# Rounding float64 weights on VectorE in pairs of operations, each pair ordered behind an hl, with a third load buffer

## The chip, the cores and the metric

One core of one Trainium2 chip runs the whole program. The metric is device time in microseconds. The kernel before was timed three times: 1932.73 us in the median, 1931.42 the lowest and 1937.19 the highest. One further execution was taken with the hardware profiler; all rows shown here come from it.

## The reference

Three stages run one after the other on 4608 tokens (8 batches of 576) of width 512.

```python
# attention: softmax of q over its last axis, of k over the sequence; out = q_s @ (k_s^T @ v)
# mixture of experts: 8 experts, the two best per token
h = np.maximum(x[mask] @ w1[e], 0.0)                       # w1[e]: 512 x 1024
out[mask] += top2_w[mask, k, None] * (h @ w2[e])           # w2[e]: 1024 x 512
# second MLP, on all tokens; w_in 512 x 2048 and w_out 2048 x 512 arrive as float64
h = x @ w_in
g = h * np.cos(h)
return (g @ w_out).astype(np.float32)
```

w_in and w_out are float64 since they are scaled by a NumPy float. The kernel reads them as pairs of 32-bit words and rounds them to float32 itself, with integer and float operations on VectorE. That rounding is what the change touches.

## The kernel before

**Arithmetic.** Every large product is made of three matmuls on float32r operands: high part times high part, low part times high part, high part times low part (`xh`, `xl` the input's parts, `w1h`, `w1l`, `w2h`, `w2l` the weights', `hh`, `hl` the hidden layer's). ScalarE (ACT) makes a high part by a copy, VectorE (DVE) or GpSimd (POOL) the low part by a subtraction.

**Stages.** Attention and routing take the first quarter of a millisecond. Then come the eight experts. The tokens of an expert are gathered in blocks of 128 rows and worked on in groups: for expert 0 groups of 2, 2, 2 and 3 blocks, for each other expert groups of 4, 3 and 2. A tenth block (`last_block`) stands in a branch that is taken only where the expert has so many tokens. The second MLP (nine groups of four blocks, "moe2") follows.

**A step.** Each expert group takes eight steps, one for each 128 hidden columns. Step f issues `mm1` (lines 745 to 764): 12 matmuls into `ph`, then ACT's relu into `hh` (L756), then DVE's `hl` (L757). `mm2` (lines 766 to 776) of a step is issued two steps later (`LAG = 2`), so TensorE (PE) has about two steps in which `hh` and `hl` may come. At the end of a group the accumulators are copied out to `ys`, the even ones on ACT (L785), the odd ones on DVE (L787), and only then may the next group's `mm2` write those PSUM banks.

**Beside each step.** Three side lines advance step by step as Python generators. `fetch` gathers the next group's rows by indirect DMA on POOL (L618) and has SP's queue spread each block in four DMAs (L645). `prep` then turns a block on DVE (L677, here called T), rounds it on ACT (L680) and subtracts on DVE (L681, here x). `w_load` brings the next expert's weights in 16 pieces: a DMA on SP into one of three `wst` buffers (L141), a copy on ACT (L136), a subtraction on POOL (L137). `convert` is the fourth line and rounds the float64 weights.

**convert.** Lines 810 to 852. There are 64 jobs of 128 x 256 numbers, 32 of w_in and 32 of w_out. A job is a load on SP (L844, 256 KB into one of two buffers `c64`, which the trace calls c), seven or eight small DVE operations on `ca` and `cb` (L821 to L825 and L831 to L833), and a store on SP (L834) to `wi_d` or `wo_d` in DRAM, from where moe2's `w_load` reads. The trace's lines of one job are, in this order, L821, L822, L823, L824, L825, L831, L832, L833: eight operations.

**What sets the order.** The program is built with a scheduler that simulates the engines' time: it puts each engine's instructions in a fixed order, and may put an instruction earlier than the Python code does where its inputs allow. Each engine, and each engine's DMA queue, then works strictly in that order: an instruction that waits holds up all behind it. `tc.issue_after(ins)` adds an edge on the same engine, so that what stands in the block comes behind `ins`; `prep` uses it for T. `after` is the list of all `hl` instructions. `convert` has no such edge.

**Buffers.** `GB` are two 128 x 512 float32 tiles, `GB[0]` and `GB[1]` (gb in the trace). Up to moe2 only `last_block` uses them, in turns, for 128 columns each (L707).

Of the kernel before, what the change touches and what calls it, by code (L numbers as in the profile page):

```python
# [10 lines left out]
F32 = mybir.dt.float32  # L11
F32R = mybir.dt.float32r
BF16 = mybir.dt.bfloat16
I32 = mybir.dt.int32
U32 = mybir.dt.uint32
AF = mybir.ActivationFunctionType
ALU = mybir.AluOpType
# [4 lines left out]
P = 128  # L22
# [5 lines left out]
def tile_attention_moe_moe2(  # L28
# [669 lines left out]
    def last_block(g):  # L698

        w1h, w1l, w2h, w2l = W[g.e % 2]  # L700
        hs = []

        def up(f):
            fs = slice(f * P, (f + 1) * P)
            ph = ps_tr("ph")
            hh, hl = HH[f % (LAG + 1)][:, LASTB], HL[f % (LAG + 1)][:, LASTB]
            t = GB[f % 2][:, :P]  # L707
            if g.nb == 2:
                for kc in range(NK):
                    nc.tensor.matmul(ph[:, :2 * P], w1h[:, kc, fs], g.xh[:, kc, 2 * P:], start=kc == 0, stop=False)  # L710
                    nc.tensor.matmul(ph[:, :P], w1l[:, kc, fs], g.xh[:, kc, 2 * P:3 * P], start=False,
                                     stop=kc == NK - 1)
                nc.scalar.activation(t, ph[:, P:2 * P], AF.Copy)
                nc.vector.tensor_tensor(t, ph[:, :P], t, op=ALU.add)
            else:
                for kc in range(NK):
                    nc.tensor.matmul(ph[:, :P], w1h[:, kc, fs], g.xh[:, kc, LASTB], start=kc == 0, stop=False)
                    nc.tensor.matmul(ph[:, :P], w1h[:, kc, fs], g.xl[:, kc, LASTB], start=False, stop=False)
                    nc.tensor.matmul(ph[:, :P], w1l[:, kc, fs], g.xh[:, kc, LASTB], start=False, stop=kc == NK - 1)
                nc.vector.tensor_copy(t, ph[:, :P])  # L720
            nc.scalar.activation(hh, t, AF.Relu)
            nc.vector.scalar_tensor_tensor(hl, t, 0.0, hh.bitcast(F32), op0=ALU.max, op1=ALU.subtract)
            hs.append((hh, hl))

        def down(f):
            hh, hl = hs[f]
            nc.tensor.matmul(acc, hh, w2h[:, f, :], start=f == 0, stop=False)
            nc.tensor.matmul(acc, hh, w2l[:, f, :], start=False, stop=False)
            nc.tensor.matmul(acc, hl, w2h[:, f, :], start=False, stop=f == NF - 1)

        with tc.If(used[g.e] > 0):
            acc = ps_acc("acc")
            for f in range(NF + LAG):
                if f < NF:
                    up(f)
                if f >= LAG:
                    down(f - LAG)
            ys = YS[0]
            nc.scalar.activation(ys, acc, AF.Copy)
            nc.scalar.dma_start(y_rows(g.e, NB - 1), ys)  # L740
# [67 lines left out]
    EMAX = float(2 ** 16 * (1 + 7 / 8 - 2.0 ** -23))  # L808

    def convert():  # L810
        pend = []
        V = nc.vector

        def half1():
            src, t, dst = pend[0]
            v2 = t.rearrange("p (n w) -> p n w", w=2)
            lo, hi = v2[:, :, 0].bitcast(U32), v2[:, :, 1]
            ab = late[1].tile([P, CW], I32, name="ca", bufs=3)
            bits = late[1].tile([P, CW], I32, name="cb", bufs=1)

            V.tensor_single_scalar(ab, hi, 0x7fffffff, op=ALU.bitwise_and)  # L821
            V.tensor_scalar(ab.bitcast(F32), ab.bitcast(F32), EMIN, EMAX, op0=ALU.max, op1=ALU.min)  # L822
            V.tensor_scalar(bits, ab, 5, 2, op0=ALU.logical_shift_left, op1=ALU.logical_shift_right)  # L823
            V.scalar_tensor_tensor(bits, ab, 0x40000000, bits, op0=ALU.bitwise_and, op1=ALU.bitwise_or)  # L824
            V.scalar_tensor_tensor(bits, hi, -2 ** 31, bits, op0=ALU.bitwise_and, op1=ALU.bitwise_or)  # L825
            return lo, bits, ab

        def half2(lo, bits, ab):
            dst = pend.pop(0)[2]
            w = ab.bitcast(F32)  # L830
            V.tensor_single_scalar(ab, bits, -2 ** 23, op=ALU.bitwise_and)  # L831
            V.scalar_tensor_tensor(w, lo, 2.0 ** -52, w, op0=ALU.mult, op1=ALU.mult)  # L832
            V.tensor_tensor(w, w, bits.bitcast(F32), op=ALU.add)  # L833
            nc.sync.dma_start(dst, w)  # L834

        jobs = []
        for src, dst in ((w_in, wi_d), (w_out, wo_d)):
            s32 = src.bitcast(I32)
            for r in range(0, src.shape[0], P):
                for c in range(0, src.shape[1], CW):  # L840
                    jobs.append((s32[r:r + P, 2 * c:2 * (c + CW)], dst[r:r + P, c:c + CW]))
        for src, dst in jobs:
            t = late[1].tile([P, 2 * CW], I32, name="c64", bufs=2)
            nc.sync.dma_start(t, src)  # L844
            pend.append((src, t, dst))
            if len(pend) == 2:
                yield
                z = half1()
                yield
                half2(*z)  # L850
        yield
        half2(*half1())

    C2 = 2.0 * math.pi - C1
    MAGIC = 1.5 * 2.0 ** 23
# [29 lines left out]
    def experts():  # L885
# [4 lines left out]
        for i in range(first, len(steps) + LAG):  # L890
# [39 lines left out]
                if f == g.nf - 1:  # L930
                    finish(pbg)
            wbg.step(2 if g.t is not None or g.e == 0 else 1)
            if g.nb > 2 or f < p0:
                cbg.step(2 if f == 0 else 1)
            if f == g.nf - 1 and nxt is not None:
                if nxt.t == 0:
                    cbg.drain()
# [217 lines left out]
```

## Time and profile before

| | |
|---|---|
| median of three runs | 1932.73 us |
| profiled execution, device time | 1936.69 us |
| its span, first to last instruction | 1934.6 us |
| PE busy | 1815.6 us, 94% |
| DVE busy | 1118.6 us, 58% |
| ACT busy | 860.6 us, 44% |
| POOL busy | 447.7 us, 23% |
| mean granted TensorE clock | 0.962 |
| DMA, mean over the span | 107 GB/s |

PE is the busy engine, so the places that matter are those where PE stands idle or where its granted clock is under full. The page's forty slices show 8s and 9s for PE between 260 and 700 us, the stretch in which the 64 jobs run, and only 9s (90% or more) from there to the last slice. Idle time of another engine costs nothing by itself; it counts only through what PE then waits for.

### The profile page before, as it was taken

The page shows a single profiled execution, that of the slowest core. Times are in us where ns is not written, and L with a number is a line of the kernel's source. Part 1 is how long each engine was busy: PE and PEld are TensorE (multiplying, and loading weights), DVE is VectorE, ACT ScalarE, POOL GpSimd, SP SyncE. Part 2 cuts the span into 40 slices and gives each one's busy share as a digit, 9 for nine tenths or more (in the row PEclk, how much of TensorE's full clock was granted, in tenths as well). Part 3 has the DMA queues.
Part 4 walks back from the last instruction along what each step waited for, and adds up shares of the span by engine and source line. Part 5 has one row for each costly group of instructions (what it writes and reads, how often), then busy time and mean ns, then how long its engine had stood idle before and what let it go on. Part 6 is the DMA issues. An engine that isn't in the chain of part 4 may idle for free. (4 is left out here: it accounts for less than half of the span.)

```text
span 1934.6 us, 27003 instructions
## 1 busy us (share of the span) xinstructions
PE 1815.6 (94%) x9738; PEld 1531.3 (79%) x9738; DVE 1118.6 (58%) x2138; ACT 860.6 (44%) x1514; POOL 447.7 (23%) x405
## 2 busy tenths in 40 slices
PE   5875988999899999999999999999999999999998
PEld 4764877788787788888888878888888888888886
DVE  4657677877767744334323357665656566665654
ACT  5542223313123132232424256666666666666654
POOL 6655033404114023041405143110101010110000
PEclk8775999999999999999999999999999999999999
DMA  9954246546545443252435342211212030201000
GB/s 269 291 168 129 79 128 206 186 142 192 150 125 182 141 132 115 79 155 81 133 92 148 98 139 65 71 28 60 56 33 66 23 88 16 72 28 49 1 23 23
DMA packets 179774, 206.18 MB, mean 107 GB/s; under 512 B 34224, under 2 KB 121264, under 8 KB 179632
## 3 DMA queue, kind: packets, MB, share of 16 engines
q1 hardware_dynamic: 160704, 152.17, 26.4%
q0 software_dynamic: 12160, 39.86, 7.1%
q10 hardware_dynamic: 6768, 12.32, 1.7%
q8 instruction: 82, 1.34, 0.3%
q14 instruction: 60, 0.49, 0.1%
HBM read 127.06 MB, written 49.43 MB: 91 GB/s over the span
## 5 line engine op out<-in xcount | busy, mean ns | idle before, releaser
L750 PE MATMUL ph<-xh,w1h 128*128 128x512 f32 (+2 forms) x1376 | 491.9, 357 | 6.9 <-DVE r L696 2.9
L752 PE MATMUL ph<-xh,w1l 128*128 128x512 f32 (+2 forms) x1376 | 491.3, 357 | 0.0
L751 PE MATMUL ph<-xl,w1h 128*128 128x512 f32 (+2 forms) x1376 | 490.6, 357 | 0.0
L774 PE MATMUL acc<-w2h,hh 128*128 128x512 f32 x1152 | 455.8, 396 | 17.1 <-DVE ys L787 9.7
L775 PE MATMUL acc<-w2l,hh 128*128 128x512 f32 x1152 | 453.3, 394 | 0.0
L776 PE MATMUL acc<-w2h,hl 128*128 128x512 f32 x1152 | 427.7, 396 | 21.5 <-DVE hl L757 19.7
L750 PEld LDWEIGHTS ph<-xh,w1h 128*128 128x128 f32 x1376 | 261.8, 190 | 47.1 <-DVE hl L757 4.0
L751 PEld LDWEIGHTS ph<-xl,w1h 128*128 128x128 f32 x1376 | 261.5, 190 | 38.2 <-DMA xl<-xg 0.8
L752 PEld LDWEIGHTS ph<-xh,w1l 128*128 128x128 f32 x1376 | 261.8, 190 | 32.1
L776 PEld LDWEIGHTS acc<-w2h,hl 128*128 128x128 f32 x1152 | 217.2, 190 | 73.7 <-DVE hl L757 26.1
L774 PEld LDWEIGHTS acc<-w2h,hh 128*128 128x128 f32 x1152 | 218.2, 189 | 65.7 <-ACT hh L756 11.1
L775 PEld LDWEIGHTS acc<-w2l,hh 128*128 128x128 f32 x1152 | 218.4, 190 | 40.4
L757 DVE SCALAR_TENSOR_TENSOR hl<-ph,hh 128x256 fp32r<-128x256 f32 (+2 forms) x200 | 107.1, 538 | 243.3 <-ACT hh L756 243.1
L756 ACT ACTIVATE hh<-ph 128x256 fp32r<-128x256 f32 (+2 forms) x200 | 93.9, 472 | 265.2 <-PE ph L752 250.8
L696 DVE SCALAR_TENSOR_TENSOR r<-r,ph 128x512 f32<-128x512 f32 x144 | 98.9, 687 | 151.4 <-ACT r L695 150.3
L618 POOL DMA_INDIRECT xg<-x_d,idx x80 | 76.8, 959 | 441.8 <-DVE xl L681 190.4
L694 ACT ACTIVATE r<-r 128x512 f32<-128x512 f32 x144 | 90.7, 630 | 151.9 <-DVE r L693 151.9
L763 DVE TENSOR_TENSOR hl<-r,hh 128x512 fp32r<-128x512 f32 x144 | 102.1, 709 | 86.4 <-ACT hh L762 86.3
L680 ACT ACTIVATE xh<-xg 128x512 fp32r<-128x512 f32 x106 | 66.7, 630 | 166.2 <-DVE xg L677 164.0
L137 POOL TENSOR_TENSOR w1l<-wst,w1h 128x512 fp32r<-128x512 f32 x80 | 104.9, 1326 | 137.9 <-ACT w1h L136 137.0
L618 POOL DMA_INDIRECT xg<-y_d,SL x36 | 34.3, 954 | 420.5 <-DVE xl L681 389.8
L692 DVE SCALAR_TENSOR_TENSOR r<-kk,ph 128x512 f32<-128x512 f32 x144 | 98.7, 685 | 51.6 <-ACT kk L691 50.0
(186 smaller groups left out, 2162.9 us busy)
## 6 DMA issues: line engine op xcount, KB each, us to landing
wst<-in_moe_w_dram SPq DMA_DIRECT2D x128, 256.0 KB
xl<-xg SPq DMA_DIRECT2D x396, 64.0 KB
y_d<-ys ACTq DMA_DIRECT2D x47, 256.0 KB
kt<-in_k_dram SPq DMA_DIRECT2D x16, 512.0 KB
vt<-in_v_dram SPq DMA_DIRECT2D x16, 512.0 KB
qt<-in_q_dram SPq DMA_DIRECT2D x16, 512.0 KB
x_d<-xs SPq DMA_DIRECT2D x32, 256.0 KB
c<-in_moe_w_in_dram SPq DMA_DIRECT2D x32, 256.0 KB
```

What stands on the lines that cost most here:

```text
L137: nc.gpsimd.tensor_tensor(lo, st, hi.bitcast(F32), op=ALU.subtract)
L618: return nc.gpsimd.indirect_dma_start(out=dst, out_offset=None, in_=src, in_offset=bass.IndirectOffsetOnAxis(ap=ix, axis=0))
L692: nc.vector.scalar_tensor_tensor(r, kk, -C1, ph, op0=ALU.mult, op1=ALU.add)
L696: nc.vector.scalar_tensor_tensor(r, r, 1.0, ph, op0=ALU.subtract, op1=ALU.mult, reverse0=True)
L750: nc.tensor.matmul(ph, w1h[:, kc, fs], g.xh[:, kc, :g.N], start=kc == 0, stop=False)
L751: nc.tensor.matmul(ph, w1h[:, kc, fs], g.xl[:, kc, :g.N], start=False, stop=False)
L752: nc.tensor.matmul(ph, w1l[:, kc, fs], g.xh[:, kc, :g.N], start=False, stop=kc == NK - 1)
L757: after.append(nc.vector.scalar_tensor_tensor(hl, ph, 0.0, hh.bitcast(F32), op0=ALU.max, op1=ALU.subtract))
L763: after.append(nc.vector.tensor_tensor(hl, r, hh.bitcast(F32), op=ALU.subtract))
L774: nc.tensor.matmul(g.acc[m], hh[:, ms], w2h[:, fr, :], start=f == 0, stop=False)
L775: nc.tensor.matmul(g.acc[m], hh[:, ms], w2l[:, fr, :], start=False, stop=False)
L776: nc.tensor.matmul(g.acc[m], hl[:, ms], w2h[:, fr, :], start=False, stop=f == g.nf - 1)
```

## The change

The eight operations of a job are issued in four pairs instead of five and three. Each pair stands in a block `held()`, an edge behind the newest `hl` that has been issued. The generator gives up control after every pair. The jobs' number, the eight operations and their sizes stay as they were. A job's store is issued after the next job's first pair. Three loads are issued at the start and then one after each job; every third of them goes to `GB[0]` (which moe2 needs later), so that there are three buffers. `last_block` now uses two halves of `GB[1]`. The rate of the generator is set anew: one to three pairs for each step, in every step of every group.

```diff
-            t = GB[f % 2][:, :P]
+            t = GB[1][:, f % 2 * P:f % 2 * P + P]
...
-        for src, dst in jobs:
-            t = late[1].tile([P, 2 * CW], I32, name="c64", bufs=2)
-            nc.sync.dma_start(t, src)
-            pend.append((src, t, dst))
-            if len(pend) == 2:
-                yield
-                z = half1()
-                yield
-                half2(*z)
-        yield
-        half2(*half1())
...
+        def load():
+            n = next(loads)
+            if n < len(jobs):
+
+                t = GB[0].bitcast(I32) if n % 3 == 2 else late[1].tile([P, 2 * CW], I32, name="c64", bufs=2)
+                nc.sync.dma_start(t, jobs[n][0])
+                ring.append(t)
+
+        def held():
+
+            return tc.issue_after(after[-1].ins)
+
+        for _ in range(3):
+            load()
+        yield
+        for _, dst in jobs:
...
+            with held():
+                V.tensor_single_scalar(ab, hi, 0x7fffffff, op=ALU.bitwise_and)
+                V.tensor_scalar(w, w, EMIN, EMAX, op0=ALU.max, op1=ALU.min)
+            yield
+            if store is not None:
+                nc.sync.dma_start(*store)
+            with held():
+                V.tensor_scalar(bits, ab, 5, 2, op0=ALU.logical_shift_left, op1=ALU.logical_shift_right)
+                V.scalar_tensor_tensor(bits, ab, 0x40000000, bits, op0=ALU.bitwise_and, op1=ALU.bitwise_or)
+            yield
+            with held():
+                V.scalar_tensor_tensor(bits, hi, -2 ** 31, bits, op0=ALU.bitwise_and, op1=ALU.bitwise_or)
+                V.tensor_single_scalar(ab, bits, -2 ** 23, op=ALU.bitwise_and)
+            yield
+            with held():
+                V.scalar_tensor_tensor(w, lo, 2.0 ** -52, w, op0=ALU.mult, op1=ALU.mult)
+                V.tensor_tensor(w, w, bits.bitcast(F32), op=ALU.add)
+            store = (dst, w)
+            load()
+            yield
+        nc.sync.dma_start(*store)
...
-            if g.nb > 2 or f < p0:
-                cbg.step(2 if f == 0 else 1)
+            busy = f < LAG or (nxt is not None and p0 <= f < p0 + nxt.nx)
+            cbg.step((1 if g.nb == 2 or f < LAG else 2) if busy else 2 if g.nb == 2 else 3)
```

Counted over the program, the jobs' operations stood, before, from the early groups of expert 0 to the end of expert 3. Now the first pair stands behind the last `hl` of expert 0, and the last pair behind the last `hl` of expert 6's three-block group.

Three places in the engines' order show the move. The first is DVE in the four-block group of expert 1, from one hl to the next but for the first three operations of before (hl_1679 to hl_1680; L821 to L833 are the rounding's operations before, L843 to L858 the same ones now). Before:

```order
L822 TENSOR_SCALAR ca<-ca 128x256
L831 TENSOR_SCALAR ca<-cb 128x256
L832 SCALAR_TENSOR_TENSOR ca<-c_4483,ca 128x256
L833 TENSOR_TENSOR ca<-ca,cb 128x256
L823 TENSOR_SCALAR cb<-ca 128x256
L824 SCALAR_TENSOR_TENSOR cb<-ca,cb 128x256
L825 SCALAR_TENSOR_TENSOR cb<-c_4559,cb 128x256
L831 TENSOR_SCALAR ca<-cb 128x256
L821 TENSOR_SCALAR ca<-c_4858 128x256
L832 SCALAR_TENSOR_TENSOR ca<-c_4559,ca 128x256
L822 TENSOR_SCALAR ca<-ca 128x256
L757 SCALAR_TENSOR_TENSOR hl_1680<-ph,hh_1677 128x512
```

Now, the same two hl:

```order
L757 SCALAR_TENSOR_TENSOR hl_1679<-ph,hh_1676 128x512
L843 TENSOR_SCALAR ca<-c_3625 128x256
L844 TENSOR_SCALAR ca<-ca 128x256
L849 TENSOR_SCALAR cb<-ca 128x256
L850 SCALAR_TENSOR_TENSOR cb<-ca,cb 128x256
L853 SCALAR_TENSOR_TENSOR cb<-c_3625,cb 128x256
L854 TENSOR_SCALAR ca<-cb 128x256
L757 SCALAR_TENSOR_TENSOR hl_1680<-ph,hh_1677 128x512
```

Between these two hl stood 14 operations of the rounding; there are 6 now, and nowhere between two hl are there more than 6.

The second place is DVE at the end of that group, in the second step of the three-block group behind it, where `ys` is copied out (L787). Before:

```order
L757 SCALAR_TENSOR_TENSOR hl_1680<-ph,hh_1677 128x384
L821 TENSOR_SCALAR ca<-c_5321 128x256
L787 COPY ys_1683<-acc 128x512
L822 TENSOR_SCALAR ca<-ca 128x256
L821 TENSOR_SCALAR ca<-c_5396 128x256
L823 TENSOR_SCALAR cb<-ca 128x256
L822 TENSOR_SCALAR ca<-ca 128x256
L787 COPY ys_1681<-acc 128x512
```

Now:

```order
L757 SCALAR_TENSOR_TENSOR hl_1680<-ph,hh_1677 128x384
L843 TENSOR_SCALAR ca<-gb_3105 128x256
L787 COPY ys_1683<-acc 128x512
L844 TENSOR_SCALAR ca<-ca 128x256
L787 COPY ys_1681<-acc 128x512
```

A job's first operation, which needs its load, still stands ahead of the first ys copy; a second job's first operation no longer stands ahead of the second one.

The third place is SP's queue at the same point of the program (the loads are L844 and now L825, the stores L834 and now L847, L645 the spreading of gathered rows, L790 the stores of ys). Before:

```order
L834 DMA wi_d<-ca 128x256
L645 DMA xl_1690<-xg_1686 32x4x128 x4
L645 DMA xl_1690<-xg_1687 32x4x128 x4
L645 DMA xh_1689<-xg_1688 32x4x128 x4
L834 DMA wi_d<-ca 128x256
L844 DMA c_5321<-in_moe_w_in_dram 128x512
L834 DMA wi_d<-ca 128x256
L844 DMA c_5396<-in_moe_w_in_dram 128x512
L790 DMA y_d<-ys_1683 128x512
```

Now:

```order
L825 DMA gb_3105<-in_moe_w_in_dram 128x512
L847 DMA wi_d<-ca 128x256
L825 DMA c_4081<-in_moe_w_in_dram 128x512
L847 DMA wi_d<-ca 128x256
L645 DMA xl_1690<-xg_1686 32x4x128 x4
L645 DMA xl_1690<-xg_1687 32x4x128 x4
L645 DMA xh_1689<-xg_1688 32x4x128 x2
L825 DMA c_4161<-in_moe_w_in_dram 128x512
L645 DMA xh_1689<-xg_1688 32x4x128 x2
L847 DMA wi_d<-ca 128x256
L790 DMA y_d<-ys_1683 128x512
```

Before, the load that the operation ahead of the ys copy reads (c_5321) stood behind the twelve DMAs of L645; now the one that it reads (gb_3105) stands ahead of them, and one more load with it.

## Rows read from the trace of the kernel before

**Rows 1.** The page: the span of the profiled execution

```profile
span 1934.6 us, 27003 instructions
```

**Rows 2.** Stretches: length, busy us (instructions) per engine, granted clock, DMA share, GB/s

```profile
264.00:309.00 45.00, 36.07 (x208) 30.38 (x206) 36.12 (x64) 14.27 (x28) 27.41 (x24) 1.00 0.63 204
309.00:338.00 29.00, 25.55 (x110) 22.50 (x111) 20.46 (x47) 6.66 (x13) 5.26 (x6) 0.88 0.68 222
338.00:460.00 122.00, 112.13 (x530) 94.52 (x531) 94.22 (x198) 32.28 (x61) 34.40 (x29) 0.96 0.54 166
402.00:450.00 48.00, 48.00 (x259) 43.27 (x259) 36.95 (x93) 9.58 (x20) 5.24 (x6) 0.95 0.44 136
460.00:580.00 120.00, 111.42 (x569) 95.91 (x568) 87.37 (x205) 31.11 (x66) 26.45 (x23) 0.97 0.51 152
580.00:700.00 120.00, 110.47 (x548) 93.74 (x547) 85.14 (x197) 31.98 (x64) 30.49 (x26) 0.97 0.51 158
700.00:820.00 120.00, 120.00 (x639) 105.42 (x638) 42.05 (x74) 37.62 (x80) 30.00 (x26) 1.00 0.34 103
```

**Rows 3.** PE's waits, 264 to 700 us: waiting, released by, us, times, longest

```profile
PE acc L776 <- DVE hl L757: 19.7, 13, 3.5
PE acc L774 <- DVE ys L787: 9.7, 3, 3.7
PE acc L774 <- ACT hh L756: 6.1, 7, 1.7
PE ph L750 <- DVE hl L757: 2.7, 3, 1.4
PE pt L671 <- DMA xg<-x_d,idx: 1.3, 1, 1.3
```

**Rows 4.** DVE in order of time: start, us, operation [idle before, releaser]

```profile
400.17 0.29 DVE L821 TENSOR_SCALAR ca<-c 128x256 int32<-128x256 int32 x1 [5.58 <-DMA c<-in_moe_w_in_dram]
400.38 0.68 DVE L787 COPY ys<-acc 128x512 f32<-128x512 f32 x1
```

**Rows 5.** SP's DMA issues in order of time, same place

```profile
387.14 5.81 SPq L645 DMA_DIRECT2D xl<-xg  x8
...
396.21 0.46 SPq L844 DMA_DIRECT2D c<-in_moe_w_in_dram  x1
```

**Rows 6.** DVE's waits for the loads, 264 to 700 us

```profile
DVE ca L821 <- DMA c<-in_moe_w_out_dram: 33.9, 23, 5.4
...
DVE ca L821 <- DMA c<-in_moe_w_in_dram: 29.6, 17, 5.6
```

**Rows 7.** Two of the eight operations: ns min/median/max, first and last start

```profile
L824 DVE SCALAR_TENSOR_TENSOR cb<-ca,cb x64: 370/426/3314, 265.8 to 692.6; 128x256 int32<-128x256 int32 x64
L831 DVE TENSOR_SCALAR ca<-cb x64: 252/289/4440, 267.1 to 694.0; 128x256 int32<-128x256 int32 x64
```

**Rows 8.** DVE in order of time, one operation

```profile
365.05 4.44 DVE L831 TENSOR_SCALAR ca<-cb 128x256 int32<-128x256 int32 x1
```

**Rows 9.** POOL in order of time, same stretch

```profile
364.42 1.10 POOL L618 DMA_INDIRECT xg<-x_d,idx  x1 [3.46 <-DVE xl L681]
365.53 1.31 POOL L137 TENSOR_TENSOR w1l<-wst,w1h 128x512 fp32r<-128x512 f32 x1
366.78 2.55 POOL L137 TENSOR_TENSOR w2l<-wst,w2h 128x512 fp32r<-128x512 f32 x2
```

**Rows 10.** DVE in order of time, one step of a two-block group, no rounding

```profile
1021.28 1.13 DVE L677 STREAM_TRANSPOSE xg<-xl 128x512 f32<-128x512 f32 x1
1023.11 0.69 DVE L681 TENSOR_TENSOR xl<-xg,xh 128x512 fp32r<-128x512 f32 x1 [0.70 <-ACT xh L680]
1023.82 0.42 DVE L757 SCALAR_TENSOR_TENSOR hl<-ph,hh 128x256 fp32r<-128x256 f32 x1
```

More of the change, by code (lines that the diff above doesn't have):

```diff
@@ L810, in convert @@
     def convert():
-        pend = []
         V = nc.vector
[L814 to L834, printed above, removed]
         jobs = []
@@ L841, in convert @@
                     jobs.append((s32[r:r + P, 2 * c:2 * (c + CW)], dst[r:r + P, c:c + CW]))
-        for src, dst in jobs:
-            t = late[1].tile([P, 2 * CW], I32, name="c64", bufs=2)
-            nc.sync.dma_start(t, src)
-            pend.append((src, t, dst))
-            if len(pend) == 2:
-                yield
-                z = half1()
-                yield
-                half2(*z)
-        yield
-        half2(*half1())
+        ring, loads, store = [], itertools.count(), None
+        def load():
[8 more added lines that the diff above has]
+            load()
+        yield
+        for _, dst in jobs:
+            v2 = ring.pop(0).rearrange("p (n w) -> p n w", w=2)
+            lo, hi = v2[:, :, 0].bitcast(U32), v2[:, :, 1]
+            ab = late[1].tile([P, CW], I32, name="ca", bufs=3)
+            bits = late[1].tile([P, CW], I32, name="cb", bufs=1)
+            w = ab.bitcast(F32)
+            with held():
[19 more added lines that the diff above has]
+        nc.sync.dma_start(*store)
     C2 = 2.0 * math.pi - C1
```

## The prediction

> **What bounds the kernel now.** I read the page first, then the table by stretches, then PE's waits, and last DVE and SP in order of time around the longest of them. The span is 1934.6 us [rows 1] and PE is its bound, so only time that PE loses can be won. The table by stretches [rows 2] shows where it loses any. In 700 to 820, an expert with no rounding beside it, PE is busy for 120.00 of 120 us at a granted clock of 1.00. In the five stretches from 264 to 700 it is idle for 8.93 + 3.45 + 9.87 + 8.58 + 9.53 = 40.4 us (length less PE's busy time), and the clock is under 1.00 in four of them. PE at a mean clock c does c of the work, so that costs 0.12 x 29 + 0.04 x 122 + 0.03 x 120 + 0.03 x 120 = 15.6 us. Together 56.0 us, and that is the most that this change can give back, since the 64 jobs run nowhere else.
>
> PE's waits in the same stretch [rows 3] name what it waited for: hl 19.7 and 2.7, the ys copy 9.7, hh 6.1, a gather 1.3. All but the last come from DVE or from ACT. DVE is not full: 94.22 of 122 us, against 42.05 of 120 without the rounding [rows 2]. So it isn't DVE's mean load, it is what stands ahead of an hl or a ys at the wrong moment. Two forms of it can be read.
>
> The first is a load that DVE waits for. At 400.17 DVE had been idle for 5.58 us for a load, at the head of a job, and the ys copy stood right behind that operation [rows 4]. The longest of PE's three waits for ys, 3.7 us [rows 3], is this one. SP shows why: its load went out at 396.21, behind the issues of L645, eight of which alone began at 387.14 and took 5.81 us [rows 5]. DVE waited for loads 33.9 + 29.6 = 63.5 us in 40 cases [rows 6].
>
> The second is mere number. An interval between two hl held up to 14 operations of 0.29 to 0.43 us each [rows 7], some 5 us, beside T, x and hl, and any of them could be drawn out: the one at 365.05 took 4.44 us [rows 8] in place of 0.29, and it ended as three POOL subtractions ended that began behind a gather (365.53 to 369.33) [rows 9].
>
> **The change, part by part.**
>
> *Number and work.* 64 jobs of eight operations before and after, so DVE's work is the same. Rounding took some 174 us of DVE: 323.3 us busy in the five stretches less 42.05/120 of their 436 us. Spread over experts 1 to 6, that is 29 us for each; with 40 of its own, DVE is busy for about 69 us of an expert's 115, 60%. In 402 to 450 DVE was at 36.95 of 48, 77%, and PE was busy for all of it; only the clock was at 0.95, behind the stall at 400 us [rows 2, 4]. So the new density by itself lies under one that PE has been seen to bear.
>
> *The edge and the pairs.* At most 6 operations now stand between two hl, some 2.2 us at 0.29 to 0.43 [rows 7]. An hl has about two steps until PE needs it. The undisturbed cost is thus hidden by that slack. The tightest place is the two-block group, into whose last steps the change newly puts pairs. There DVE without rounding runs T 1.13, waits 0.70 for ACT, x 0.69, hl 0.42: a step of 2.88 us from hl to hl less the overlap of neighbours, and DVE is what paces it [rows 10]. A pair takes 0.58 to 0.85 us and stands between T and x, so it falls into the 0.70 us that DVE idles there: at most 0.15 us a step, four steps a group, which the slack takes up. If that cover were gone (the pair ahead of T instead), it would be 0.7 x 4 = 2.8 us for each expert.
>
> *Drawn-out operations.* These stay: w_load's 16 subtractions on POOL still fall into the four-block group, with up to six operations beside each. Price for an expert from below: 0, as in 700 to 820. From above: the loss of the three experts that had rounding before, (9.87 + 8.58 + 9.53 + 4.9 + 3.6 + 3.6) / 3 = 13.4 us. By the order, the four-block group of expert 1 has 34 operations where it had 66, and no late load among them; I take 1 us, near the lower row, so 6 us for six experts. The Trainium skill, "SBUF — State Buffer", section "SBUF: two separate sides", speaks of the pair of ports that DVE and GpSimd share as an exclusive lock held for one whole instruction. By that, an operation of DVE would lose no more than the rest of one POOL instruction, 1.3 us, every interval would fit into its step, and the six experts would cost 0 instead of 6: 1880. The trace differs: 4.44 us is three of POOL's instructions in a row [rows 8, 9], so the measured length holds in my sum.
>
> *The third buffer and SP.* A load is now issued at the end of a job for the third one after, so it goes out some eight pairs ahead of its use, which at one to three pairs a step is at least three steps. Landing takes about 4 us (issued 396.21, used 400.17 [rows 4, 5]). In SP's order the load for the operation ahead of the ys copy stands in front of L645's twelve DMAs. So the 63.5 us of DVE's waits should nearly go, and the 9.7 us for ys with them. Loads and stores on SP keep their number and size. What comes late next is the weights' own chain (SP, ACT, POOL) with hh behind it on ACT: 6.1 us of PE's waits, partly there without any rounding in the way; I leave it in the 1 us for each expert.
>
> *The early groups and the clock.* Nothing of the rounding is left ahead of expert 0's last hl but three loads. Of the 12.4 us idle there the gather's 1.3 stays, and about as much again for ACT waiting for weights: 3 us. The clock is under 1.00 only in stretches with some per cent of PE idle or right behind them, and 1.00 in 700 to 820 [rows 2]; without the idle time I let it cost nothing.
>
> *last_block* in halves of one tile: same operations, same lengths, 0. The bound is one wait of a small operation in each of 8 columns and 4 experts, 0.3 x 32 = 10 us, if the two halves waited for each other; their instructions wait for the same engines as before, so I take 0.
>
> *Sum.* 1936.7 us (the profiled execution) - 56.0 + 6 + 3 = 1889.7. That execution lies 4.0 us above the median of the three runs, so against the median 1886.
>
> **Rivals.** *Half comes back.* Drawn-out operations and ACT's waits for weights cost each of six experts about 5 us with the clock, as hh's and half of hl's waits did (6.1 + 11 us over some three and a half experts [rows 3]): 6 x 5 in place of 6, so 1910. For it: the POOL chain is untouched, and three experts more carry the rounding. Against it: 402 to 450.
>
> *Slower, by the head of a job.* A pair that waits for its load holds up hl and ys behind it, now in six experts. If SP stays behind with its L645 issues, so that loads still come late by 5.58 us ahead of ys in every expert, each loses what the three lost, 13.4: 6 x 13.4 + 3 - 56 = +27, 1960. It decides from (56 - 3) / 6 = 8.8 us for each expert. Against it: the load's new place in SP's order, and that the first three experts can hardly lose as much with half the operations.
>
> *It does nothing.* The scheduler could have kept the old density; the order shows that it hasn't. The time would be 1933.
>
> **The numbers.** Forecast 1886 with 0.72; half back 0.20; slower 0.04; nothing 0.04. The range goes from 1878 (1 us lost in all) to 1912, with the half-back case's 1910 in it. A difference under 0.3% (6 us) can't be told from no change. Faster 0.92, same 0.04, slower 0.04.
>
> **What would show it.** Right: in 264 to 1030 of the new profile PE idle in all under 12 us, clock 1.00 in each expert, DVE's wait for loads under 10 us, no wait for ys over 1 us, DVE near 60% in experts 1 to 6. Drawn-out operations will still be there, but PE doesn't wait for them. Wrong: waits of PE for hl in the four-block groups of experts 4 to 6, where there were none; the clock at its lower level (1.2 GHz) behind them; a head operation idle for a load ahead of ys.

## The result, and the profile after

The changed kernel takes 1886.02 us in the median (1881.85 to 1887.52) against 1933.51 (1931.42 to 1937.19) for the kernel before, taken again beside it: a ratio of 0.9749, 95% interval 0.9733 to 0.9766. The profiled execution took 1886.52 us. The page gives its span, 49.9 us less than [rows 1]:

```profile
span 1884.7 us, 27071 instructions
```

The table by stretches, with the columns of [rows 2]. The six stretches from 336.20 on are experts 1 to 6, each from its first hl to the next expert's; the jobs now stand there:

```profile
264.00:309.00 45.00, 40.54 (x237) 36.53 (x235) 7.89 (x18) 15.88 (x31) 27.93 (x24) 0.96 0.61 183
...
336.20:434.30 98.10, 97.95 (x496) 85.09 (x495) 66.64 (x137) 29.69 (x56) 30.05 (x26) 1.00 0.53 162
434.30:547.70 113.40, 113.40 (x597) 99.54 (x597) 70.18 (x152) 35.25 (x72) 29.59 (x27) 1.00 0.47 144
547.70:660.30 112.60, 112.60 (x594) 98.84 (x593) 70.39 (x153) 35.26 (x72) 30.76 (x28) 1.00 0.48 146
660.30:772.80 112.50, 112.50 (x594) 98.76 (x593) 69.95 (x152) 35.34 (x72) 30.10 (x27) 1.00 0.48 147
772.80:886.50 113.70, 113.70 (x599) 99.71 (x598) 70.25 (x153) 35.41 (x72) 31.58 (x28) 1.00 0.47 146
886.50:984.70 98.20, 98.05 (x497) 85.19 (x496) 58.98 (x116) 30.00 (x55) 29.89 (x27) 1.00 0.49 151
...
1080.00:1115.00 35.00, 28.19 (x118) 21.25 (x117) 19.00 (x20) 24.08 (x42) 25.76 (x22) 1.00 0.66 188
```

PE is busy for all but 0.15 us at most of each of these experts, where [rows 2] had 8.58 to 9.87 us of idle time in each of experts 1 to 3, and the clock is 1.00 in each. DVE is busy for 68% of expert 1 (66.64 of 98.10 us) and for 60 to 63% of the others. Nearly all idle time that is left ahead of expert 7 is the 4.46 us in the first row, and there the clock is at 0.96.

PE's waits from 260 to 1130 us (waiting, released by, us, times, longest), to be laid beside [rows 3]:

```profile
PE ph L750 <- DVE r L696: 4.1, 3, 2.8
PE acc L774 <- ACT hh L756: 3.2, 2, 2.7
PE acc L774 <- ACT hh L762: 1.7, 1, 1.7
PE pt L671 <- DMA xg<-x_d,idx: 1.3, 1, 1.3
PE acc L776 <- DVE hl L763: 0.9, 1, 0.9
```

The waits for an hl of L757 and for ys, 19.7, 2.7 and 9.7 us in [rows 3], have no row any more; hh is down from 6.1 to 3.2 us. The rows for r, for the other hh (L762) and for the other hl (L763) belong to moe2.

The place of [rows 4], DVE in order of time at the first ys copies of expert 1:

```profile
376.98 0.28 DVE L843 TENSOR_SCALAR ca<-gb 128x256 int32<-128x256 int32 x1
377.37 0.69 DVE L787 COPY ys<-acc 128x512 f32<-128x512 f32 x1
...
378.75 0.69 DVE L787 COPY ys<-acc 128x512 f32<-128x512 f32 x1 [0.48 <-PE acc L776]
```

The job's first operation still stands ahead of the copy, but it no longer waits for its load. Nor does any other: DVE's waits for the loads, 63.5 us in [rows 6], have no row in this trace. The drawn-out operations are still there, as this group shows beside the one of [rows 7] (ns min/median/max):

```profile
L854 DVE TENSOR_SCALAR ca<-cb x64: 286/294/1384, 337.4 to 954.6; 128x256 int32<-128x256 int32 x64
```

Its longest took 1.38 us, where 4.44 us stood before. Counted over all operations of the rounding, 31 lasted over 0.4 us longer than the median of their form (33 before), but none lasted over 1.7 us (9 before).

The following times between stages are differences of the starts of certain hl (L757) in each trace, in us. The first stage ends with the fifteenth hl of expert 0, which starts just ahead of the rounding; expert 0's time is counted from there, and the last stage takes in the second MLP. The column of experts 1 to 3 is where [rows 2] showed most of the loss. Each ratio is to runs of the kernel before taken beside that kernel.

| kernel | median, us | ratio to before, 95% interval | up to expert 0's 15th hl | rest of expert 0 | experts 1 to 3 | experts 4 to 6 | from expert 7 on |
|---|---|---|---|---|---|---|---|
| before | 1933.51 | | 257.4 | 87.6 | 367.4 | 324.4 | 897.9 |
| after | 1886.02 | 0.9733 to 0.9766 | 260.1 | 76.2 | 324.0 | 324.4 | 900.0 |
| edge alone | 1883.35 | 0.9689 to 0.9765 | 256.5 | 76.1 | 324.0 | 324.5 | 898.7 |
| no edge | 1945.99 | 1.0033 to 1.0066 | 260.2 | 84.7 | 376.5 | 324.5 | 897.9 |
| two buffers | 1883.84 | 0.9689 to 0.9765 | 259.9 | 76.3 | 323.9 | 324.3 | 899.1 |
| third buffer alone | 1944.34 | 1.0032 to 1.0067 | 258.1 | 83.9 | 377.8 | 324.4 | 898.3 |
| three experts | 1908.89 | 0.9844 to 0.9879 | 259.7 | 77.6 | 349.2 | 324.3 | 899.9 |
| operations twice | 1891.71 | 0.9748 to 0.9789 | 260.7 | 76.8 | 327.0 | 326.1 | 900.9 |
| no rounding | 1884.82 | 0.9727 to 0.9762 | 258.6 | 76.0 | 324.2 | 324.5 | 899.8 |
| no rounding, three experts | 1885.03 | 0.9722 to 0.9763 | 259.3 | 75.2 | 323.3 | 324.4 | 900.3 |
| held combine | 1879.90 | 0.9697 to 0.9740 | 258.2 | 74.1 | 323.7 | 324.4 | 895.9 |
| held split | 1879.63 | 0.9686 to 0.9733 | 261.3 | 72.0 | 322.8 | 325.3 | 896.5 |
| held combine and split | 1874.24 | 0.9673 to 0.9715 | 255.7 | 71.8 | 322.8 | 325.3 | 895.4 |
| edges alone | 1877.27 | 0.9683 to 0.9727 | 258.9 | 72.3 | 322.7 | 325.3 | 895.0 |

The first of these stages lies ahead of everything that the change moves, and it varies by 5.6 us from one trace to the next (255.7 to 261.3). So a few us between two single traces say nothing unless the stage is named.

### The profile page after: what moved, and what is told of

Its sections match the earlier page's. It is cut to its first block, busy times and chain, and to the rows that moved or that the text cites. A ratio compares the mean times of both kernels' runs of the same rounds, so it can differ in the third digit from the quotient of the medians.

```text
span 1884.7 us, 27071 instructions
## 1 busy us (share of the span) xinstructions
PE 1795.7 (95%) x9738; PEld 1521.2 (81%) x9738; DVE 1105.8 (59%) x2138; ACT 861.6 (46%) x1514; POOL 447.7 (24%) x405
## 5 line engine op out<-in xcount | busy, mean ns | idle before, releaser
L776 PE MATMUL acc<-w2h,hl 128*128 128x512 f32 x1152 | 422.6, 391 | 1.5 <-DVE hl L763 0.9
L757 DVE SCALAR_TENSOR_TENSOR hl<-ph,hh 128x256 fp32r<-128x256 f32 (+2 forms) x200 | 107.8, 540 | 273.9 <-ACT hh L756 264.1
L763 DVE TENSOR_TENSOR hl<-r,hh 128x512 fp32r<-128x512 f32 x144 | 103.9, 721 | 85.1 <-ACT hh L762 85.0
```

The costliest lines, as they stand in the source:

```text
L757: after.append(nc.vector.scalar_tensor_tensor(hl, ph, 0.0, hh.bitcast(F32), op0=ALU.max, op1=ALU.subtract))
L763: after.append(nc.vector.tensor_tensor(hl, r, hh.bitcast(F32), op=ALU.subtract))
L776: nc.tensor.matmul(g.acc[m], hl[:, ms], w2h[:, fr, :], start=False, stop=f == g.nf - 1)
```

## The experiments

**Is it the edge?** The changed kernel with `held()` empty: pairs, new rate, third buffer and the code of the loads all stay.

```diff
         def held():
-            return tc.issue_after(after[-1].ins)
+            return ExitStack()
```

> The changed kernel without the edge behind hl; pairs, rate, third buffer as changed. By the order the scheduler then puts up to 20 operations of the rounding between two hl and begins in expert 0's early groups again. Theory A (what stands ahead of an hl or a ys decides, and the edge sets it): 1915 to 1935 us, PE's waits for hl back at 10 us or more. Theory B (late loads at the head of a job decide, and the third buffer cures them): 1886 to 1900, waits for loads few and PE's waits with them.

Measured: 1945.99 us (1940.94 to 1946.88), ratio 1.005: slower than the kernel before, and above both theories' ranges. One row of the rounding's first operation (ns min/median/max, first and last start) tells where it stands:

```profile
L843 DVE TENSOR_SCALAR ca<-c x43: 244/294/1385, 267.3 to 651.7; 128x256 int32<-128x256 int32 x43
```

The code issues its pairs up to expert 6, yet they run from 267.3 to 651.7 us, about as before (264.6 to 684.0): without the edge the scheduler brings them forward, up to 20 of them between two hl. DVE's waits at the head of a job and then PE's, 240 to 1080 us:

```profile
DVE ca L843 <- DMA wi_d<-ca: 22.9, 16, 3.6
DVE ca L843 <- DMA wo_d<-ca: 21.1, 17, 3.2
```

```profile
PE acc L776 <- DVE hl L757: 17.6, 12, 3.8
PE acc L774 <- DVE ys L787: 15.6, 3, 5.3
```

In 33 of the 64 jobs the first operation now waits for the store of an earlier job to free its tile `ca`, 44.0 us, in place of the 63.5 us for loads, and PE waits for ys for 15.6 us where it was 9.7. The order on SP went back as well: at the place of [rows 5] the job's load went out at 395.36 us and the store that the job waits for at 395.99, both behind the twelve DMAs of L645 (from 387.60), and DVE was idle for 2.71 us ahead of the ys copy. The waits for an hl have another cause in the main: four of them, 11.5 of the 17.6 us, stand behind operations that were drawn out by 2.8 to 4.1 us, with no wait for a DMA since the hl before. All of the change but the edge is worth less than nothing.

**Is the edge enough?** The kernel before with the edge around its two halves of a job, five and three operations, two buffers, the old code of loads and stores and the old rate.

```diff
-                z = half1()
+                with tc.issue_after(after[-1].ins):
+                    z = half1()
...
-            V.tensor_single_scalar(ab, bits, -2 ** 23, op=ALU.bitwise_and)
-            V.scalar_tensor_tensor(w, lo, 2.0 ** -52, w, op0=ALU.mult, op1=ALU.mult)
-            V.tensor_tensor(w, w, bits.bitcast(F32), op=ALU.add)
+            with tc.issue_after(after[-1].ins):
+                V.tensor_single_scalar(ab, bits, -2 ** 23, op=ALU.bitwise_and)
+                V.scalar_tensor_tensor(w, lo, 2.0 ** -52, w, op0=ALU.mult, op1=ALU.mult)
+                V.tensor_tensor(w, w, bits.bitcast(F32), op=ALU.add)
```

> The kernel before with nothing but the edge: five and three operations, each piece behind the newest hl; two buffers, old rate. By the order at most 8 operations between two hl, jobs up to expert 6. Theory A: most of the gain, 1886 to 1898 us. Theory B: the loads are as late as before, 1915 to 1933.

Measured: 1883.35 us (1881.49 to 1883.97), the changed kernel's time and better than theory A's range. The first operation of the rounding, and DVE's only waits for loads (240 to 1080 us):

```profile
L821 DVE TENSOR_SCALAR ca<-c x64: 247/284/1196, 333.3 to 938.2; 128x256 int32<-128x256 int32 x64
```

```profile
DVE ca L821 <- DMA c<-in_moe_w_out_dram: 0.9, 1, 0.9
...
DVE ca L821 <- DMA c<-in_moe_w_in_dram: 0.5, 1, 0.5
```

The jobs' first operations now run from 333.3 to 938.2 us, at the old code's own rate: the edge alone also spreads them over six experts. The waits for loads fall from 63.5 to 1.4 us with two buffers. The edge moved the order on SP too, though it stands on DVE's operations alone. At the first ys copies of expert 1, where the load stood behind L645's DMAs in [rows 5], it now goes out ahead of them (L845 is the load here):

```profile
365.20 0.33 SPq L845 DMA_DIRECT2D c<-in_moe_w_in_dram  x1
...
366.10 5.65 SPq L645 DMA_DIRECT2D xl<-xg  x8
```

Drawn-out operations are here too: five lasted from 2.8 to 3.6 us, one each in experts 1, 3, 4, 5 and 6, and these experts take as long as in the changed kernel to 0.1 us.

**Is the third buffer needed with the edge?** The changed kernel, with all loads to the two buffers `c64` and two of them at the start.

```diff
-                t = GB[0].bitcast(I32) if n % 3 == 2 else late[1].tile([P, 2 * CW], I32, name="c64", bufs=2)
+                t = late[1].tile([P, 2 * CW], I32, name="c64", bufs=2)
...
-        for _ in range(3):
+        for _ in range(2):
```

> The changed kernel with two load buffers instead of three; DVE's order is the same, a load now goes out one job (four pairs) ahead instead of two. Theory A: DVE waits for loads some 10 to 30 us in all, but an expert keeps its time: 1884 to 1892 us. Theory B: waits for loads come back at over 40 us, with ys waits of 3 us in most experts: 1900 to 1920.

Measured: 1883.84 us (1883.14 to 1885.31). It is not needed: the stages are the changed kernel's to 0.9 us, and the ratios' intervals overlap. DVE waits for no load here either, where 10 to 30 us had been expected.

**Does it help without the edge?** The kernel before with every third load to `GB[0]`, three loads ahead, and `last_block` in halves of `GB[1]`.

```diff
-            t = late[1].tile([P, 2 * CW], I32, name="c64", bufs=2)
+            t = GB[0].bitcast(I32) if n % 3 == 2 else late[1].tile([P, 2 * CW], I32, name="c64", bufs=2)
...
-            if len(pend) == 2:
+            if len(pend) == 3:
...
-            t = GB[f % 2][:, :P]
+            t = GB[1][:, f % 2 * P:f % 2 * P + P]
...
```

> The kernel before with nothing but the third load buffer (and last_block in halves of one tile): no edge, five and three operations. By the order up to 20 operations between two hl, as without it. Theory A: at most the ys waits go, 9.7 us and some clock: 1918 to 1933 us. Theory B: most of the gain, 1886 to 1900.

Measured: 1944.34 us (1941.53 to 1948.38), ratio 1.005, again above both ranges. DVE's waits, 240 to 1080 us:

```profile
DVE ca L821 <- DMA c<-in_moe_w_out_dram: 11.6, 5, 3.4
DVE ca L821 <- DMA wo_d<-ca: 11.1, 11, 3.1
DVE ca L821 <- DMA wi_d<-ca: 10.6, 10, 3.4
...
DVE ca L821 <- DMA gb<-in_moe_w_in_dram: 4.7, 3, 2.8
DVE ca L821 <- DMA gb<-in_moe_w_out_dram: 2.9, 2, 2.3
...
DVE ca L821 <- DMA c<-in_moe_w_in_dram: 2.7, 2, 2.1
```

The waits for loads fall from 63.5 to 21.9 us (11.6 + 4.7 + 2.9 + 2.7), and 21.7 us of waits for stores (11.1 + 10.6) come in their place, at the same operation, a job's first. The buffer doesn't help without the edge, and experts 1 to 3 take 10.4 us longer than before.

One more number of the traces ties these kernels together: the time from a load's issue on SP to the start of the operation that reads it, in the median of the 64 jobs. It was 3.5 us before, 4.9 and 4.7 us in the two kernels without the edge that have three buffers, 9.9 and 10.9 us in the two with the edge and two buffers, and 19.7 us in the changed kernel. The edge gives a load more time than the third buffer does.

**How much is the spread?** The changed kernel at twice the rate: up to 12 operations between two hl, all behind an edge, and the jobs stand in three experts, no thinner than before (512 operations from 324.7 to 659.5 us, before from 264.6 to 707.0).

```diff
-            cbg.step((1 if g.nb == 2 or f < LAG else 2) if busy else 2 if g.nb == 2 else 3)
+            cbg.step(2 * ((1 if g.nb == 2 or f < LAG else 2) if busy else 2 if g.nb == 2 else 3))
```

> The changed kernel at twice the rate: the edge kept, the jobs in experts 1 to 3, up to 12 operations between two hl, as dense as before. Theory A1 (the edge decides by itself: what stands behind an hl can't hold up that hl, and PE's two steps of slack take the rest): at most 10 us over the changed kernel, 1884 to 1896 us. Theory A2 (the number between two hl decides, and the edge acts only by spreading the jobs): most of the loss of before back in experts 1 to 3, 1910 to 1935.

Measured: 1908.89 us (1907.26 to 1912.87), between the two. So pacing without a lower density gives 1.4%, and the spread over six experts gives the other 1.1%. Experts 2 and 3 by stretches, the two largest of PE's waits, and DVE's waits for stores (264 to 1060 us):

```profile
447.00:569.00 122.00, 116.30 (x588) 98.80 (x587) 102.89 (x242) 33.71 (x71) 30.64 (x26) 0.97 0.57 172
569.00:687.00 118.00, 115.11 (x593) 99.81 (x592) 91.75 (x215) 34.37 (x72) 30.52 (x27) 0.99 0.52 160
```

```profile
PE acc L776 <- DVE hl L757: 7.6, 6, 3.0
PE acc L774 <- ACT hh L756: 5.9, 5, 2.6
```

```profile
DVE ca L843 <- DMA wo_d<-ca: 9.3, 7, 2.6
...
DVE ca L843 <- DMA wi_d<-ca: 5.7, 5, 2.9
```

PE loses 5.70 and 2.89 us with the clock at 0.97 and 0.99; DVE is busy for 84% of expert 2 and still waits 15.0 us for stores. The next runs take these two apart.

**A full DVE without those waits.** The changed kernel, the first six operations of each job done twice (the second time on the same data): 384 more operations, again up to 12 between two hl.

```diff
                 V.tensor_single_scalar(ab, hi, 0x7fffffff, op=ALU.bitwise_and)
                 V.tensor_scalar(w, w, EMIN, EMAX, op0=ALU.max, op1=ALU.min)
+                V.tensor_single_scalar(ab, hi, 0x7fffffff, op=ALU.bitwise_and)
+                V.tensor_scalar(w, w, EMIN, EMAX, op0=ALU.max, op1=ALU.min)
...
```

> The changed kernel with the first six of each job's eight operations done twice (the second time to the same result): 896 operations instead of 512, up to 12 between two hl, over six experts. DVE is then busy for about 75 to 80% of an expert. Theory A1: under 5 us over the changed kernel, 1884 to 1891. Theory A2: several us in each of six experts, 1910 or more.

Measured: 1891.71 us (1887.58 to 1893.72), 5.7 us over the changed kernel (the ratios' intervals overlap) and just above theory A1's range; the table finds 3.0 us in experts 1 to 3 and 1.7 in 4 to 6. Experts 2 and 3 of it by stretches:

```profile
435.00:549.00 114.00, 113.67 (x597) 99.13 (x596) 92.80 (x218) 34.84 (x72) 30.32 (x26) 1.00 0.46 144
549.00:664.00 115.00, 113.71 (x596) 98.90 (x595) 93.94 (x218) 34.94 (x73) 31.64 (x27) 1.00 0.47 144
```

DVE is busy for 81 and 82% of the time, more than in any stretch of [rows 2], and PE loses 0.33 and 1.29 us. DVE waits for no load and no store there.

**No rounding at all.** The changed kernel with only the first and the seventh of a job's eight operations, so that loads and stores stay.

```diff
-                V.tensor_scalar(w, w, EMIN, EMAX, op0=ALU.max, op1=ALU.min)
+                pass
...
-            with held():
-                V.tensor_scalar(bits, ab, 5, 2, op0=ALU.logical_shift_left, op1=ALU.logical_shift_right)
-                V.scalar_tensor_tensor(bits, ab, 0x40000000, bits, op0=ALU.bitwise_and, op1=ALU.bitwise_or)
...
-            with held():
-                V.scalar_tensor_tensor(bits, hi, -2 ** 31, bits, op0=ALU.bitwise_and, op1=ALU.bitwise_or)
-                V.tensor_single_scalar(ab, bits, -2 ** 23, op=ALU.bitwise_and)
...
-                V.tensor_tensor(w, w, bits.bitcast(F32), op=ALU.add)
```

> The changed kernel without six of a job's eight operations: each job is one load, one mask, one product and one store, so the weights of the second MLP are not the rounded ones. It shows what the rounding still costs. If it costs nothing any more, 1880 to 1888 us, as the changed kernel; if the 6 us that the prediction left to it are there, 1878 to 1882.

Measured: 1884.82 us (1884.70 to 1887.64). Experts 1 to 6 take as long as with the rounding: it costs nothing any more.

**The same at twice the rate.** The edit of the three-expert run made in the kernel without rounding.

```diff
-            cbg.step((1 if g.nb == 2 or f < LAG else 2) if busy else 2 if g.nb == 2 else 3)
+            cbg.step(2 * ((1 if g.nb == 2 or f < LAG else 2) if busy else 2 if g.nb == 2 else 3))
```

> The kernel of e3 (twice the rate, jobs in experts 1 to 3) with two of a job's eight operations left, so that the second MLP's weights are not the rounded ones; loads and stores at twice the rate as in e3. If e3's 22 us over the changed kernel come from DVE's own work and its drawn-out operations, they go: 1883 to 1889 us. If they come from the loads and stores at twice the rate (SP holding up the weights' pieces, operations waiting for stores), at least half stays: 1896 to 1909.

Measured: 1885.03 us (1884.19 to 1886.44). DVE's waits for stores (264 to 1060 us), and expert 2:

```profile
DVE ca L843 <- DMA wi_d<-ca: 7.6, 6, 3.6
...
DVE ca L843 <- DMA wo_d<-ca: 4.3, 3, 3.7
```

```profile
435.00:549.00 114.00, 114.00 (x600) 99.98 (x599) 53.66 (x108) 35.14 (x72) 30.67 (x26) 1.00 0.60 184
```

DVE waits for stores for 11.9 us, near the 15.0 us of the three-expert run, at a higher DMA share (0.60 against 0.57), and PE is never idle in that expert. So neither the traffic nor the waits for stores cost anything by themselves on a DVE half full. But this run took away the drawn-out operations with the work: none of its 128 operations lasted over 1.7 us, six of the three-expert run's 512 did. What PE's six waits for an hl stood behind in the three-expert run can be read in its trace. Three of them, 4.6 of the 7.6 us, stand behind drawn-out operations alone. This is the longest, PE and then DVE ahead of it:

```profile
479.97 0.79 PE L776 MATMUL acc<-w2h,hl 128*128 128x512 f32 x1 [2.96 <-DVE hl L757]
```

```profile
474.68 3.30 DVE L853 SCALAR_TENSOR_TENSOR cb<-c,cb 128x256 int32<-128x256 int32 x1
478.01 1.30 DVE L854 TENSOR_SCALAR ca<-cb 128x256 int32<-128x256 int32 x1
```

DVE works without a pause from the hl at 468.60 us to the late one at 479.24; between them stand eight operations of the rounding, T and x, and four of the eight are drawn out, by 5.8 us in all. The other three waits, 3.0 us, stand behind waits for stores. (PE's idle time in experts 1 to 3 of that run is 5.8 + 5.7 + 2.9 = 14.4 us, so the waits for hl are half of it.) So at twice the rate both forms that the prediction had read come back beside the edge, the drawn-out operations in the larger part. The run with the operations done twice has as many operations between two hl and drawn-out ones as well (four of 1.9 to 3.1 us), but PE waited for hl for 1.1 us only; why it got off so lightly was not settled.

**The same edge at other places.** Most of what PE still waits for in the changed kernel stands behind other early instructions. ACT in order of time, ahead of a late hh of expert 0:

```profile
290.70 0.63 ACT L136 ACTIVATE w1h<-wst 128x512 fp32r<-128x512 f32 x1 [2.02 <-DMA wst<-in_moe_w_dram]
...
293.59 0.63 ACT L136 ACTIVATE w1h<-wst 128x512 fp32r<-128x512 f32 x1 [1.40 <-DMA wst<-in_moe_w_dram]
294.13 0.36 ACT L756 ACTIVATE hh<-ph 128x256 fp32r<-128x256 f32 x1
```

ACT stands idle for 2.02 and 1.40 us at weight copies whose loads have not landed, with hh behind them. After expert 7, PE is idle for 6.81 us in 1080 to 1115 (last row of the stretches). DVE in order of time there:

```profile
1096.57 0.75 DVE L640 SCALAR_TENSOR_TENSOR xg<-gb,W,xg 128x512 f32<-128x512 f32 x1 [1.18 <-DMA gb<-y_d,SL]
1099.60 2.87 DVE L640 SCALAR_TENSOR_TENSOR xg<-gb,W,xg 128x512 f32<-128x512 f32 x1 [2.28 <-ACT xg L639]
```

The combine (L640) waits for rows of y and for ACT, which scales them, and stands ahead of the hl and the r that PE waits for in the list above. In the changed kernel, the weight copies got an edge behind the newest hh, the combine one behind the newest hl, each alone and both together.

```diff
-                nc.vector.scalar_tensor_tensor(a, b, W2[:, c, 1:2], a, op0=ALU.mult, op1=ALU.add)
+                with tc.issue_after(after[-1].ins):
+                    nc.vector.scalar_tensor_tensor(a, b, W2[:, c, 1:2], a, op0=ALU.mult, op1=ALU.add)
...
-            nc.scalar.activation(hi, st, AF.Copy)
+            with tc.issue_after(hhs[-1].ins) if hhs else ExitStack():
+                nc.scalar.activation(hi, st, AF.Copy)
...
-            nc.scalar.activation(hh, ph, AF.Relu)
+            hhs.append(nc.scalar.activation(hh, ph, AF.Relu))
```

> One half of v2: the edge on the combining of gathered rows (L640) alone. Expected to keep v2's gain at the change to the second MLP and from there on (v2: 801.9 us from expert 7's last hl to the end, changed kernel 807.2) and none of that in the early groups: 1879 to 1883 us. If v2's gain is the weight copies' alone: 1884 to 1888.

> The other half of v2: the edge on ACT's weight copies (L136) alone. Expected to keep v2's gain in the early groups (40.1 us in place of 45.5): 1877 to 1883 us. If v2's gain is the combining's alone: 1884 to 1888.

> The changed kernel with the same edge at two more places where its profile shows PE idle: the combining of gathered rows on DVE (L640) behind the newest hl, and the weight copies on ACT (L136) behind the newest hh. If the cause is the same there, the 2.7 us for hh in the early groups and most of 6.8 us at the change to the second MLP go: 1876 to 1882 us. If these waits come from the gathers and the weight loads themselves, 1884 to 1888.

Measured: 1879.90 us for the combine (1878.09 to 1882.41), 1879.63 for the weight copies (1876.05 to 1881.63), 1874.24 for both (1872.82 to 1879.35), just below its range and with a ratio whose interval lies wholly under the changed kernel's. The interval of each alone reaches the changed kernel's, so neither is proved alone. Nor do the stages divide between them as expected: the weight copies' edge alone also shortens the last stage by 3.5 us (the combine's by 4.1), and the combine's edge alone also shortens expert 0 by 2.1 (the weight copies' by 4.2). With both, the stretches that answer to the first and the last of those of after:

```profile
264.00:309.00 45.00, 44.78 (x262) 40.64 (x261) 12.34 (x20) 13.51 (x28) 13.85 (x14) 1.00 0.40 128
...
1072.00:1110.00 38.00, 37.30 (x162) 29.87 (x162) 24.73 (x28) 27.09 (x47) 20.38 (x17) 1.00 0.43 121
```

PE loses 0.22 us in the early groups where 4.46 were lost, and 0.70 us at the change to moe2 where 6.81 were. Not all of that is won: the whole last stage is 4.6 us shorter, as some idle time comes later in moe2 instead (11.57 us behind that stretch, 9.54 in the changed kernel).

The last run is the kernel before with all three edges and nothing else: the diffs of the edge alone and of these two.

> The kernel before with nothing but edges: e5 (rounding behind the newest hl, two buffers, five and three operations) and the two edges of v2. If pairs and third buffer give nothing, as e5 and e2 say, the same as v2: 1871 to 1879 us. If they help beside the other edges: over 1880.

Measured: 1877.27 us (1875.89 to 1879.72). Its interval overlaps that of the best version, so here too no gain of the pairs, the third buffer or the new rate is shown.

## Why the prediction was right, and where it was not

The time came as forecast and the loss was where the prediction had put it: 47.0 us were to go, 50.2 went between the two profiled executions. That the medians agree to 0.02 us (1886 and 1886.02) is luck, since the stages differ from the forecast by more and partly cancel:

| stage | forecast, us | measured, us |
|---|---|---|
| up to expert 0's 15th hl | 0 | +2.7 |
| rest of expert 0 | -15.9 + 3 = -12.9 | -11.4 |
| experts 1 to 3 | -40.1 + 3 = -37.1 | -43.4 |
| experts 4 to 6 | +3 | 0.0 |
| from expert 7 on | 0 | +2.1 |

The signs that were to show it right all came: from 264 to 1030 us PE is idle for 4.9 us, the clock is 1.00 in each of experts 1 to 6, DVE waits for no load and PE for no ys. None of the signs of being wrong came.

- **What PE loses, 56.0 us at most in the five stretches.** Right in size. Experts 1 to 3 gave back 43.4 us (367.4 to 324.0), where idle time and clock had been put at 28.0 + 12.1 = 40.1; where the other 3.3 come from was not settled. Expert 0 gave back 11.4 of a forecast 12.9: 3 us were to stay there, and 4.46 us of idle time and 0.04 x 45 = 1.8 us of clock did.
- **Drawn-out operations, 6 us.** This is the mis-sized term. It is 0: experts 4 to 6, which had no rounding before and have it now, take 324.4 us both times, and without any rounding experts 1 to 6 take the same time to 0.2 us. Operations are drawn out as often as before, and the slack of about two steps that the prediction gave an hl takes that up, not only the changed kernel's 1.4 us but also the 2.8 to 3.6 us of the kernel with the edge alone. The price hangs on the density: with up to twelve operations between two hl, in three experts, drawn-out ones cost PE 4.6 us of waits again beside the edge.
- **The third buffer and SP's order.** The forecast held, its cause did not. The waits for loads and for ys did go, but the prediction credited the buffer and the place of the loads on SP. With two buffers they go as well; with the buffer and without the edge the kernel is slower than before. The loads' place on SP was never varied by itself: at the first ys copies of expert 1 the load goes out ahead of L645's DMAs in the kernels with the edge and behind them in those without it, whichever code of the loads they have. It is part of what the edge does. What a load needs is time between issue and use (3.5 us in the median before, 9.9 with the edge and the same two buffers), and that comes from holding back the operation that uses it.
- **The density.** "60%" was 60 to 68 (the prediction's 174 us of rounding should read 323.3 - 152.8 = 170.5, and its 14 operations between two hl were 15 in one interval; neither changes the argument), and that PE bears it was right by a wide margin: 81 and 82% cost 0.33 and 1.29 us in an expert. But density was treated as something that the new rate sets. It is the edge that does: the old rate, with the edge, gives the same six experts, and the new rate without it the same three.
- **The slower rival**, a job's head that holds up hl and ys, is real. It came in both kernels without the edge, with 44.0 us of waits for stores in the one and 21.7 us for stores and 21.9 us for loads in the other, and at 1946 and 1944 us, not at 1960.
- **Half comes back.** It did not: from 264 us on PE waits for no hl of L757, and for hh only ahead of expert 1.
- **The pairs in the two-block group, last_block in halves.** 0 as forecast: experts 4 and 5, which have both, take what they took.
- **Not forecast:** 2.7 us more ahead of expert 0's fifteenth hl and 2.1 us more from expert 7 on. The first is within the scatter of that stage; the second was not settled, though the edge on the combine gives back 4.1 us of that stage and the one on the weight copies 3.5.

Why the scheduler puts a job's head so early without the edge was not measured. That it takes a DMA as landed sooner than the chip does would fit all runs: more buffers only moved waits from the loads to the stores.

## What to carry to other kernels

Where a scheduler may bring side work forward, tie each piece to the step beside which it belongs, on the same engine: here that one edge was the whole gain of 2.5%, and it also decided how far the work was spread. Before adding a buffer for a late transfer, look whether the instruction that waits for it stands too early; a third buffer without the edge only turned part of the waits for loads into waits for stores, and the kernel was 0.5% slower. How full the side engine is says little: beside a VectorE that was busy for 82% of the time, TensorE lost 1.29 us in an expert. Look rather at what stands between two of the instructions that it waits for: up to eight operations, some of them drawn out, vanished in two steps of slack, and at up to twelve TensorE waited again, 1.1 us in one run and 7.6 us in another.

## What the runs showed of the hardware

An operation of DVE on SBUF alone can last as long as several instructions of POOL. The longest, in the run without the edge, in order of time on DVE and then on POOL:

```profile
614.05 4.56 DVE L858 TENSOR_TENSOR ca<-ca,cb 128x256 f32<-128x256 f32 x1
```

```profile
613.56 0.96 POOL L618 DMA_INDIRECT xg<-x_d,idx  x1 [2.37 <-DVE ca L854]
614.54 2.54 POOL L137 TENSOR_TENSOR w1l<-wst,w1h 128x512 fp32r<-128x512 f32 x2
617.04 1.28 POOL L137 TENSOR_TENSOR w2l<-wst,w2h 128x512 fp32r<-128x512 f32 x1
```

It began while POOL was gathering, and ended at 618.61, 0.3 us after the third of POOL's subtractions ended (617.04 + 1.28 = 618.32), with no gap for it between them; [rows 8, 9] show the same. In the kernel before, 7 of the 9 operations over 1.7 us began during a gather with subtractions right behind it and the other two during a subtraction. Of those that began during a gather, 44 with nothing right behind it stayed short, and so did 8 that had ended before the gather did. This shows when it happens, not what holds the operation. The Trainium skill, "SBUF — State Buffer", section "SBUF: two separate sides", has DVE and GpSimd share a pair of ports under a lock that is held for one whole instruction. The operation's 4.56 us, against some 0.4 undisturbed, hold three subtractions of about 1.27 us and not one, so the measured length decides.
